# Float64 weights converted in pairs with ScalarE's help, and attention scores in four column-tiled strips

## The chip, the core and the metric

The kernel runs on one core of a Trainium2 chip. The metric is the device time of one execution in microseconds (us); the time of a kernel is the median of several executions. The engines are called as in the profile: PE (TensorE, matmuls), PEld (its weight loads), DVE (VectorE), ACT (ScalarE), POOL (GpSimd) and SP (SyncE, which here only issues DMAs). ACT and POOL have DMA queues too.

## What is computed

A linear recurrence over 768 steps (4 sequences, 8 heads, head size 48), a gated up/down layer with weights that come as float64, and a top-1 mixture of 8 experts. The reference, cut to what matters:

```python
# recurrence; complex decay a, only the real part of the state is read
for t in range(S):
    new_re = ar * S_re - ai * S_im
    new_im = ar * S_im + ai * S_re
    S_re, S_im = new_re + k[t] (x) v[t], new_im
    y[t] = q[t] @ S_re
x = (x @ w_a * (x @ w_b)) @ w_out          # 384 -> 1536 -> 384, float64 weights
e = argmax(x @ w_gate); p = softmax(x @ w_gate)[e]
out = p * (max(x @ w1[e], 0) @ w2[e])      # 8 experts, 384 -> 1024 -> 384
```

## The kernel before

**Stages.** The 3072 tokens go in 12 batches j of 256 tokens, three batches to a sequence, each batch in two chunks c of 128 tokens. A first phase takes each batch through the recurrence and the gated layer; a second one, from about 604 us on, runs the experts on tokens sorted by expert. The second phase is the same in both kernels but for the eviction of the very last tile.

**The recurrence of a chunk.** DVE, ACT and POOL make decayed keys and queries, which are written to DRAM and read back transposed as kT and qT by small DMAs (L1300; those of qT are issued by ACT, those of kT by SP). PE then makes, for each group hg of four heads, the scores `sc` (L1349: four matmuls 96x128 by 96x128 in fp32, which the trace shows as two records each); DVE multiplies them with a causal mask into `sm` (L1353); PE transposes the keys, `kn` (L1358, four heads a bank), which ACT copies to SBUF (L1363); PE makes `y` (L1388) from `sm` and v and from the state T and qT, in four column tiles of 32, and `kv` (L1408), the new addition to the state, also in column tiles of 32. ACT and DVE turn y into the high and low part of x (L1399, L1402), DVE updates the state from kv. Two small DVE copies (L1293, `column`) put the decay of a chunk beside q and A. The PSUM tiles of sc, kn, kv, of the folded gate weights (wt_p, wg_p) and of the expert counts (rk_p) share one ring of three banks, "sc".

**The gated layer.** Batch 0 runs in plain fp32 (`up32` L979, `down32` L985) since its weights are not yet split; later batches take f32r products in three terms, high x high, high x low and low x high (`up` L971 from xH, xL; `down` L1014 from gH, gL). Weights are cut into 12 slices f of 128 columns of w_a and w_b, and 128 rows of w_out. A float64 matrix slice of 128x384 is loaded by SP as pairs of 32-bit words (`raw`, L888, L890) and made into fp32 by three DVE operations: exponent and upper mantissa shifted (L897), low bits or-ed in (L900), sign or-ed in (L903). This is `conv`, 36 times. For w_out PE also transposes the slice and folds the gate weights into eight more columns (wt_p L916, wg_p L926, with ACT's copies L920 and L929). Later `parted` splits each slice into a high part (ACT, L953) and a low one: ACT writes -a into wL (L946) and a DMA of POOL's adds a rounded to it (L949).

**Order.** All of phase 1 is put in order by the class `Plan`. Each piece of work is added with an engine, a weight (its planned duration), a due time `at`, and what it reads and writes. `run` plays five queues forward with these weights and always emits the ready piece with the earliest due time. The table `TIMES` shifts due times by kind, with a pair (shift, stretch). Instructions then stand on each engine in the order emitted, and an engine works its own list strictly in that order. DMAs of SP and ACT carry one of eight semaphores in turn, so a DMA also waits for the one eight issues before it (DMAHW0 to 7 in the listings below).

Of the kernel before, what the change touches and what calls it, by code (L numbers as in the profile page):

```python
# [16 lines left out]
HP = 64  # L17
DM, DFF = 384, 1536
NF = DFF // 128
# [14 lines left out]
FH = 4  # L34
MH = (20.0, 3.0, 26.0, 3.0)
SPLIT = (70.0, 1.51, 6.0)
FIRST = (6, 3)
# [10 lines left out]
    ('pre', 0, 1, 0): (-32.6, 1),  # L48
    ('pre', 0, 1, 1): (18.2, 2.16),
    ('pre', 0, 0, 3): (6.7, 4),  # L50
    ('pre', 0, 0, 4): (12.1, 1),
    ('pre', 0, 1, 2): (-17.5, 1),
    ('pre', 0, 1, 3): (-26.8, 1),
    ('attn', 0, 'PE'): (-31.9, 1),
    'load': (-11.6, 1),
    'conv': (2, 1),
    'fold': (15.3, 0.43),
    ('pre', 1, 0, 0): (-21.7, 1),
    ('pre', 1, 0, 1): (-21.2, 1),
    ('turn', 1, 0): (-24.5, 1),  # L60
    ('pre', 1, 0, 3): (9, 1.54),
    ('attn', 1, 'PE'): (8, 1.03),
    ('gate', 0, (0,)): (-8.7, 1.46),
    ('down', 0, (0,)): (35, 1),
    ('up', 0, (0, 1)): (27, 1),
    ('down', 0, (0, 1)): (16.9, 0.28),
    'less': (-1.8, 0.8),
    'high': (-0, 0.89),
    ('pre', 2, 0, 0): (-70.8, 1),
    ('pre', 2, 0, 1): (-3.6, 0.35),  # L70
    ('pre', 2, 0, 2): (-32.9, 1),
    ('pre', 2, 0, 4): (-43.4, 1),
    ('up', 1): (35.8, 0.57),
    ('gate', 1): (-26.5, 0.3),
    ('attn', 2, 'PE'): (40.4, 0.51),
    ('v', 3): (-41, 1),
    ('down', 2): (15.5, 0.93),
    ('attn', 3, 'PE'): (33.2, 0.77),
    ('pre', 4, 0, 0): (39.6, 1),
    ('pre', 4, 0, 1): (-35.1, 1),  # L80
    ('pre', 4, 0, 3): (-31.5, 1),
    ('up', 3): (-5.1, 0.16),
    ('gate', 3): (93.4, 1),
    ('down', 3): (-11.7253, 1.2931),
    ('attn', 4, 'PE'): (4.8735, 1),
    ('attn', 4, 'DVE'): (-34.6, 1),
    ('attn', 4, 'ACT'): (-22.9, 1),
    ('up', 4): (-11.3, 1),
    ('gate', 4): (-41.3, 1),
    ('down', 4): (-9.1, 1),  # L90
# [5 lines left out]
F64_HI = float(np.uint32((1150 << 20) | 0xFF000).view(np.float32))  # L96

# [363 lines left out]
def fast(tc, q, k, v, a_re, a_im, w_a, w_b, w_out, w_gate, w1, w2, out, dram, x2d):  # L461
# [5 lines left out]
    with ExitStack() as mctx, ExitStack() as ctx:  # L467
# [9 lines left out]
        p_sc = sctx.enter_context(tc.tile_pool(name="p_sc", bufs=3, space=bass.MemoryType.PSUM))  # L477
# [376 lines left out]
        def pair(nm, f):  # L854
            return ("ab", f) if nm != "o" else ("o", f // 2)
# [4 lines left out]
        def width(nm):  # L860
            return 384 + (NE if nm == "o" else 0)
# [736 lines left out]
```

## Time and profile before

| | us |
|---|---|
| median of 3 runs | 896.99 (896.51 to 898.57) |
| the profiled execution | 897.96 |
| its span | 896.2 |
| PE busy in the span | 850.6 (95%) |
| DVE / ACT / POOL busy | 562.2 / 479.7 / 318.3 |

The profiled execution is 0.97 us above the median and 1.76 us longer than its span. PE's busy share counts overlapping records of a pipelined engine as one stretch, so 95% says that PE had work in flight for all but 45.6 us. In the profile's 40 slices PE stands at 0 and 3 in the first two and at 9 from then to the last but one; the granted clock is full in every slice. The chain of work that ended last is PE for 92% of the span.

### The profile page before, as it was taken

What the parts mean: (1) busy time and instruction counts of PE and PEld (TensorE: products, weight loads), DVE (VectorE), ACT (ScalarE), POOL (GpSimd) and SP (SyncE); (2) the same over time, 40 slices, a digit from 0 to 9 for tenths busy, and PEclk for the clock granted to TensorE, in tenths of its full rate; (3) what the DMA queues carried; (4) which work ended last, traced back from release to release, by engine and by line L of the source; (5) the groups of instructions that cost most, each with busy time, mean ns of one, the idle gap of its engine ahead of it and who ended that gap; (6) DMA issues with size and microseconds to landing.
All of it is one profiled execution on the core that took longest, in us unless ns stands there. A gap on an engine that the chain in (4) does not pass through costs nothing.

```text
span 896.2 us, 20677 instructions
## 1 busy us (share of the span) xinstructions
PE 850.6 (95%) x8186; PEld 815.9 (91%) x8186; DVE 562.2 (63%) x1285; ACT 479.7 (54%) x915; POOL 318.3 (36%) x309
## 2 busy tenths in 40 slices
PE   0399999999999999999999999999999999999997
PEld 0387899999999999999999999999999999999996
DVE  6999996775647567484939576345563655455541
ACT  6478787674746456564646473224452544444441
POOL 2341441323363636354353545221123223234111
PEclk9999999999999999999999999999999999999999
DMA  9999975242324272734354453403444454454510
GB/s 253 267 273 259 231 147 151 76 112 66 115 49 131 62 221 46 193 92 124 117 154 132 93 156 81 125 2 111 156 116 128 143 161 136 144 171 125 163 61 24
DMA packets 133017, 120.28 MB, mean 134 GB/s; under 512 B 35964, under 2 KB 127434, under 8 KB 132911
## 3 DMA queue, kind: packets, MB, share of 16 engines
q1 hardware_dynamic: 121519, 100.60, 39.7%
q0 software_dynamic: 9664, 17.47, 8.4%
q8 instruction: 66, 1.08, 0.5%
q10 hardware_dynamic: 1728, 0.79, 0.4%
q14 instruction: 40, 0.33, 0.1%
HBM read 82.48 MB, written 10.61 MB: 104 GB/s over the span
## 4 chain that ended last, share of the span: by engine, by line
PE 92%; DVE 3%; DMA 3%; SPq 1%; ACT 1%; issue 0%; POOL 0%; ACTq 0%; POOLq 0%
PE ab_p L971 31%; PE o L1014 16%; PE o L810 13%; PE h_p L778 12%; PE sc_p L1349 4%; PE y_p L1388 4%; PE ab_p L979 3%; PE o L985 2%; PE kv_p L1408 2%; PE kn_p L1358 1%; PE tn_p L755 1%; DMA q<-in_q_dram 1%; DMA qT<-A 1%; DMA raw<-in_moe_w_dram 1%; DMA raw<-in_moe_w_a_dram 1%; SPq L1138 0%
## 5 line engine op out<-in xcount | busy, mean ns | idle before, releaser
L971 PE MATMUL ab_p<-xH,wL 128*128 128x256 f32 x792 | 221.7, 280 | 0.0
L971 PEld LDWEIGHTS ab_p<-xH,wL 128*128 128x128 f32 x792 | 148.9, 188 | 0.0
L1005 POOL TENSOR_TENSOR gL<-g,gH 128x256 fp32r<-128x256 f32 x96 | 80.0, 835 | 172.3 <-ACT gH L1001 165.6
L994 ACT COPY g<-ab_p 128x256 f32<-128x256 f32 x132 | 48.9, 371 | 136.8 <-PE ab_p L971 124.0
L997 DVE TENSOR_TENSOR g<-g,ab_p 128x256 f32<-128x256 f32 (+1 forms) x148 | 60.5, 409 | 94.0 <-ACT g L994 92.0
L971 PE MATMUL ab_p<-xH,waH 128*128 128x256 f32 x396 | 114.0, 288 | 0.0
L971 PE MATMUL ab_p<-xL,waH 128*128 128x256 f32 x396 | 111.4, 281 | 0.0
L971 PE MATMUL ab_p<-xL,wbH 128*128 128x256 f32 x396 | 110.9, 280 | 0.0
L971 PE MATMUL ab_p<-xH,wbH 128*128 128x256 f32 x396 | 110.8, 280 | 0.0
L1014 PE MATMUL o<-woH,gH 128*128 128x392 f32 x264 | 96.5, 365 | 0.0
L1014 PE MATMUL o<-wL,gH 128*128 128x392 f32 x264 | 90.0, 341 | 0.0
L1014 PE MATMUL o<-woH,gL 128*128 128x392 f32 x264 | 89.9, 341 | 0.0
L810 PE MATMUL o<-w2H,h 128*128 128x384 f32 (+3 forms) x312 | 86.4, 340 | 0.0
L778 PE MATMUL h_p<-sH,w1H 128*128 128x256 f32 (+6 forms) x240 | 77.4, 322 | 0.2 <-DVE hL L789 0.2
L778 PE MATMUL h_p<-sH,w1L 128*128 128x256 f32 (+6 forms) x240 | 76.9, 321 | 0.0
L778 PE MATMUL h_p<-sL,w1H 128*128 128x256 f32 (+6 forms) x240 | 76.8, 320 | 0.0
L971 PEld LDWEIGHTS ab_p<-xH,waH 128*128 128x128 f32 x396 | 74.8, 189 | 0.9 <-issue 0.2
L1001 ACT ACTIVATE gH<-g 128x256 fp32r<-128x256 f32 x132 | 54.5, 413 | 38.5 <-DVE g L997 35.3
L971 PEld LDWEIGHTS ab_p<-xL,waH 128*128 128x128 f32 x396 | 74.7, 189 | 0.4
L971 PEld LDWEIGHTS ab_p<-xH,wbH 128*128 128x128 f32 x396 | 75.0, 189 | 0.0
L971 PEld LDWEIGHTS ab_p<-xL,wbH 128*128 128x128 f32 x396 | 74.8, 189 | 0.0
L824 POOL DMA_INDIRECT out_dram<-ye,ids x29 | 29.9, 1032 | 112.1 <-ACT ye L823 99.9
(211 smaller groups left out, 2135.8 us busy)
## 6 DMA issues: line engine op xcount, KB each, us to landing
raw<-in_moe_w_dram SPq DMA_DIRECT2D x64, 384.0 KB, 3.4
x2d<-x SPq DMA_DIRECT2D x24, 196.0 KB, 3.3
q<-in_q_dram SPq DMA_DIRECT2D x24, 192.0 KB, 4.5
v<-in_v_dram SPq DMA_DIRECT2D x24, 192.0 KB, 4.1
raw<-in_moe_w_a_dram SPq DMA_DIRECT2D x12, 384.0 KB, 6.8
raw<-in_moe_w_b_dram SPq DMA_DIRECT2D x12, 384.0 KB, 5.4
raw<-in_moe_w_out_dram SPq DMA_DIRECT2D x12, 384.0 KB, 7.4
wL<-a POOLq DMA_DIRECT2D x24, 192.0 KB, 6.8
```

What stands on the lines that cost most here:

```text
L778: nc.tensor.matmul(out=t, lhsT=lh[:, o:o + 128], rhs=rh[:, kk], start=n == 0, stop=n == 8)
L810: nc.tensor.matmul(out=G["o", c], lhsT=lh, rhs=rh, start=f == 0 and n == 0, stop=f == NH - 1 and n == len(ops) - 1)
L824: d = nc.gpsimd.indirect_dma_start(out, bass.IndirectOffsetOnAxis(ap=ids[0:r, c:c + 1], axis=0), y[0:r], None, bounds_check=NT - 1, oob_is ...
L971: nc.tensor.matmul(out=t[:, i], lhsT=lh[:, kk * 128:(kk + 1) * 128], rhs=rh[:, kk], start=n == 0, stop=n == 8)
L979: nc.tensor.matmul(out=t[:, i], lhsT=A32[nm, f][:, kk * 128:(kk + 1) * 128], rhs=xT["F", 0][:, kk, cs[0]:cs[0] + len(cs)].rearrange("p c t ...
L994: nc.scalar.copy(out=G["g", j, f], in_=G["ab", j, f][:, 0])
L997: nc.vector.tensor_tensor(out=G["g", j, f], in0=G["g", j, f], in1=G["ab", j, f][:, 1], op=ALU.mult)
L1001: nc.scalar.activation(out=G["H", j, f], in_=G["g", j, f], func=ACTF.Copy)
L1005: eng.tensor_tensor(out=G["L", j, f], in0=G["g", j, f], in1=G["H", j, f].bitcast(F32), op=ALU.subtract)
L1014: nc.tensor.matmul(out=G["o", j, c], lhsT=lh[:, c * C:(c + 1) * C], rhs=rh, start=f == first and n == 0, stop=f == last and n == 2)
L1349: nc.tensor.matmul(out=S["p", hg][:, h], lhsT=pq["k", j][:, hg * 4 + h, c, :], rhs=pq["q", j][:, hg * 4 + h, c, 0:C], start=True, stop=True)
L1388: nc.tensor.matmul(out=t[q4 * 32:q4 * 32 + 32, kk], lhsT=a, rhs=b, start=f0, stop=f1)
```

## The change

1. **Conversion in pairs** (`conv`). The slices of w_a and w_b of one f lie side by side in a tile "ab" of 768 columns; w_out keeps its own. The three DVE operations become one ACT operation and two of DVE: ACT scales the low word into a float whose low mantissa bits carry it (`tail`, L934), DVE shifts the high word and xors (`body_`, L937), then or-s it with a constant and xors (`head`, L940). 24 units (12 of 768, 12 of 384 columns) instead of 36.
2. **Splitting** (`parted`). For f below 9 ACT makes the high part in one operation and DVE subtracts (`taken`, L1008); no ACT negation and no POOL DMA. For f from 9 on the old way stays, with 768 columns for ab.
3. **Scores in strips**, for batches j from 3 on (`sc`, L1454). The keys of a head are taken in four strips of 32, and a strip's matmul covers only the queries from its own first one on: 128, 96, 64 and 32 columns. The strips of the four heads of a group go to four different column tiles. Scores lie in two banks kept for them, zeroed once (`emptied`); since a head's strips are rotated by r, v has three rotated copies `vrot`, loaded by six small DMAs of SP a chunk, and the mask is a rotated 128x4x128 tile in bf16, built on POOL at the start.
4. **Banks.** From j=3 on kn, kv and rk share the single bank that is left (ring "s1").
5. **Sessions**, from j=3 on. Column-tiled work stands together on PE: the scores of chunk 0; y and kv of chunk 0 with the scores of chunk 1; y and kv of chunk 1.
6. **Smaller things.** The `column` copies go from DVE to ACT; the last tile's eviction is one ACT operation instead of a half on ACT and a half on DVE; the PSUM pool of phase 2 is opened anew; a new `TIMES` table (43 entries became 61), so that the order of phase 1 changes throughout.

```diff
-    for hg in range(2):
-        add("PE", 0.9, at_(sc, hg), qk + [("kT", c), ("qT", c)], [("sc_p", j, c, hg)], take="sc")
...
+    for b in range(0, C, STRIP):
+        for r in range(4):
+            a = (b + r * STRIP) % C
+            nc.tensor.matmul(out=t[a:a + STRIP, r, b:C], lhsT=pq["k", j][:, hg * 4 + r, c, b:b + STRIP], rhs=pq["q", j][:, hg * 4 + r, c, b:C], start=True, stop=True)
...
+    if c == 0:
+        add("PE", 1.54, both, qk + [("kT", 0), ("qT", 0)], P_)
+    else:
+        rest, after, r_, w_ = pending.pop()
...
+        add("PE", 4.05 - (0.9 if first_b else 0), joined, r_ + qk + [("kT", 1), ("qT", 1)], w_ + P_, take=ring(j))
...
+        add("PE", 2.7 if not last else 1.95, lambda rest=rest: [f() for f in rest], r_, w_, **({} if last else dict(take=ring(j))))
...
-        P = Plan({"sc": 3})
+        P = Plan({"sc": 3, "s1": 3 - KEPT})
...
+            def tail():
+                held()
+                nc.scalar.activation(out=K["a"].bitcast(F32), in_=K["lo"], func=ACTF.Copy, scale=TAIL[0], bias=TAIL[1])
+            def body_():
+                nc.vector.scalar_tensor_tensor(out=K["a"], in0=K["hi"], scalar=3, in1=K["a"], op0=ALU.logical_shift_left, op1=ALU.bitwise_xor)
+            def head():
+                nc.vector.scalar_tensor_tensor(out=K["a"], in0=K["hi"], scalar=0x7FFFFFFF, in1=K["a"], op0=ALU.bitwise_or, op1=ALU.bitwise_xor)
...
+            def taken():
+                nc.vector.tensor_tensor(out=W["L", nm, f], in0=A32[nm, f], in1=W[nm, f][0], op=ALU.subtract)
...
-                        nc.vector.tensor_copy(out=(ld[x, j] if x == "q" else PT[x, j])[:, :, lo:hi, C:C + 1], in_=T("A")[:, :, :, C - 1:C])
+                        nc.scalar.copy(out=(ld[x, j] if x == "q" else PT[x, j])[:, :, lo:hi, C:C + 1], in_=T("A")[:, :, :, C - 1:C])
...
-                            elif e == NE - 1 and c == nt - 1:
-                                nc.scalar.activation(out=y[0:r, 0:DM // 2], in_=G["o", c][:, 0:DM // 2], func=ACTF.Copy, scale=gt[0:r, c])
-                                nc.vector.tensor_scalar(out=y[0:r, DM // 2:DM], in0=G["o", c][:, DM // 2:DM], scalar1=gt[0:r, c], scalar2=None, op0=ALU.mult)
...
     'load': (-11.6, 1),
-    'conv': (2, 1),
+    'load': (3.846, 0.5624),
+    'conv': (119.1, 0.419),
```

How instructions stand now at three places. (waits DMAHW3) names the semaphore of the DMA that a DMA waits for.

SP's queue in the first 40 us, before: the transposed keys of chunk 0, then the next weight loads (raw).

```order
L1300 DMA kT<-Bt 16x8x128 [waits DMAHW0_49]
L1300 DMA kT<-k 16x8x128 [waits DMAHW1_49,DVE_49]
L1300 DMA kT<-k 16x8x128 [waits DMAHW3_49]
L1300 DMA kT<-k 16x8x128 [waits DMAHW4_49]
L890 DMA raw<-in_moe_w_a_dram 128x3x256 [waits DMAHW6_49]
```

And after:

```order
L1390 DMA kT<-Bt 16x8x128 [waits DMAHW2_49]
L915 DMA raw<-in_moe_w_a_dram 128x3x256 [waits DMAHW3_49]
L1390 DMA kT<-k 16x8x128 [waits DMAHW5_49,DVE_49]
L1390 DMA kT<-k 16x8x128 [waits DMAHW7_49]
L1390 DMA kT<-k 16x8x128 [waits DMAHW0_49]
```

A weight load now stands between the two groups of transposed keys, and it takes the semaphore DMAHW3.

ACT's queue at the same place, before: the last three transposed queries of chunk 0 (qT<-q) between small activations.

```order
L1300 DMA qT<-q 16x8x129 [waits DMAHW2_49,DVE_49]
L1275 ACTIVATE X<-X 128x3x128 [waits DVE_49]
L1300 DMA qT<-q 16x8x129 [waits DMAHW5_49]
L1187 ACTIVATE X<-X,biases 128x3x128 [waits Activation_49]
L1187 ACTIVATE X<-X 128x3x128 [waits DVE_49]
L1300 DMA qT<-q 16x8x129 [waits DMAHW7_49]
```

And after:

```order
L975 COPY a_294<-wg_p 128x8 [waits PE_49]
L1390 DMA qT<-A 16x8x129 [waits DMAHW4_49]
L1390 DMA qT<-q 16x8x129 [waits DMAHW6_49]
L1286 ACT_TABLE_LOAD
L1390 DMA qT<-q 16x8x129 [waits DMAHW1_49]
L1390 DMA qT<-q 16x8x129 [waits DMAHW3_49]
```

The last of the three now waits for DMAHW3, which the weight load above holds.

PE in the steady part, batch 3, before: y and kv of a chunk, with nothing of the next chunk beside them (o is the down projection, ab_p the up projection).

```order
L1388 MATMUL y_p<-sm,v_182 32x128 x16
L1408 MATMUL kv_p<-v_182,kn 32x48 x24
L1014 MATMUL o_2413<-woH_1554,gH 128x392
L1014 MATMUL o_2413<-wL,gH 128x392
```

And after, where the scores of the next chunk follow as strips, 16 matmuls for each group of four heads:

```order
L1498 MATMUL y_p<-sm,vr_169 32x128 x8
L1518 MATMUL kv_p<-v_164,kn 32x48 x24
L1454 MATMUL scores<-qT,kT 32x128 x4
L1454 MATMUL scores<-qT,kT 32x96 x4
L1454 MATMUL scores<-qT,kT 32x64 x4
L1454 MATMUL scores<-qT,kT 32x32 x4
L1454 MATMUL scores<-qT,kT 32x128 x4
L1454 MATMUL scores<-qT,kT 32x96 x4
L1454 MATMUL scores<-qT,kT 32x64 x4
L1454 MATMUL scores<-qT,kT 32x32 x4
L1076 MATMUL o_2322<-woH_1620,gH 128x392
```

Counted over the whole of PE's list, the column-tiled places of batches 3 to 11 (a run of y, kv or strips with no other matmul inside) are 32 before and 27 after; the 36 groups of old scores stand apart from them.

## Rows read from the trace of the kernel before

**Rows 1.** Windows of the span: stretch, length, busy us by engine (instructions)

```profile
39.36:118.47 79.11, 77.44 (x1018) 64.26 (x1019) 75.38 (x160) 61.92 (x130) 29.22 (x31) 1.00 1.05 252
186.00:604.20 418.20, 418.20 (x4615) 407.38 (x4617) 259.31 (x582) 224.37 (x408) 184.00 (x168) 1.00 0.40 109
```

**Rows 2.** Timeline of the start: start, length, engine, line, operation, tiles, count

```profile
33.02 0.58 ACTq L1300 DMA_DIRECT2D qT<-q  x1
33.42 0.59 SPq L890 DMA_DIRECT2D raw<-in_moe_w_a_dram  x1
39.41 0.56 ACTq L1300 DMA_DIRECT2D qT<-A  x1
39.36 3.76 PE L1349 MATMUL sc_p<-qT,kT 96*128 96x128 f32 x16
```

**Rows 3.** DMA issues, 30 to 46 us: tiles, queue, count, KB, us to landing

```profile
qT<-q ACTq DMA_DIRECT2D x6, 64.5 KB, 4.3
```

**Rows 4.** Timeline of PE, one group of old scores among down-projection matmuls

```profile
146.66 1.05 PE L1349 MATMUL sc_p<-qT,kT 96*128 96x128 f32 x8
147.47 0.42 PE L1014 MATMUL o<-woH,gH 128*128 128x392 f32 x1
147.73 0.34 PE L1014 MATMUL o<-wL,gH 128*128 128x392 f32 x1
```

**Rows 5.** Timeline of PE, the end of a y and the matmul behind it

```profile
389.69 0.40 PE L1388 MATMUL y_p<-sm,v 128*32 128x128 f32 x8
389.91 0.40 PE L1388 MATMUL y_p<-qT,T 96*32 96x128 f32 x8
390.24 0.44 PE L1014 MATMUL o<-woH,gH 128*128 128x392 f32 x1
```

**Rows 6.** Timeline of PE, a kv between up and down projections

```profile
393.26 0.28 PE L971 MATMUL ab_p<-xL,wbH 128*128 128x256 f32 x1
393.38 0.28 PE L971 MATMUL ab_p<-xH,wL 128*128 128x256 f32 x1
393.58 0.88 PE L1408 MATMUL kv_p<-v,kn 128*32 128x48 f32 x48
394.39 0.45 PE L1014 MATMUL o<-woH,gH 128*128 128x392 f32 x1
394.69 0.34 PE L1014 MATMUL o<-wL,gH 128*128 128x392 f32 x1
394.87 0.34 PE L1014 MATMUL o<-woH,gL 128*128 128x392 f32 x1
```

**Rows 7.** Timeline of PE, the folded gate weights: 24 records of 8 columns

```profile
67.70 0.38 PE L926 MATMUL wg_p<-wg,wt 128*32 128x8 f32 x24
68.00 0.60 PE L985 MATMUL o<-a,g 128*128 128x392 f32 x1
```

**Rows 8.** Groups, DVE to 118 us, ACT to 140: busy us, mean ns

```profile
L903 DVE SCALAR_TENSOR_TENSOR a<-raw,a 128x384 uint32<-128x384 uint32 x36 | 19.4, 549 | 0.0
L897 DVE TENSOR_SCALAR a<-raw 128x384 uint32<-128x384 uint32 x36 | 13.7, 401 | 1.0 <-DMA raw<-in_moe_w_a_dram 1.0
L1221 DVE SCALAR_TENSOR_TENSOR X<-X,re 128x768 f32<-128x768 f32 x2 | 1.9, 946 | 0.0
L1187 ACT ACTIVATE X<-X 128x768 f32<-128x768 f32 x6 | 5.1, 844 | 0.0
```

**Rows 9.** Timeline of the last eviction, and of a whole one

```profile
881.25 0.58 ACT L823 ACTIVATE ye<-o,gt 128x384 f32<-128x384 f32 x1 [1.12 <-PE o L810]
889.62 0.42 ACT L818 ACTIVATE ye<-o,gt 120x192 f32<-120x192 f32 x1 [7.79 <-PE o L810]
890.08 0.42 DVE L819 TENSOR_SCALAR ye<-o,gt 120x192 f32<-120x192 f32 x1 [4.01 <-ACT ye L818]
```

**Rows 10.** Timeline of PE and ACT, a transposed key group and its copy

```profile
257.69 0.49 PE L1358 MATMUL kn_p<-ident,kT 96*128 96x96 f32 x4
258.23 0.48 ACT L1363 COPY kn<-kn_p 128x384 f32<-128x384 f32 x1 [0.32 <-PE kn_p L1358]
```

More of the change, by code (lines that the diff above doesn't have):

```diff
@@ L79 @@
[L79 to L90, printed above, removed]
+    ('pre', 0, 1, 0): (70.2, 1),
+    ('pre', 0, 0, 2): (-165.1, 1),
+    ('turn', 0, 0): (-39.1, 1),
@@ new lines @@
+    ('up', 0, (0, 1)): (-121.9, 1),
+    'less': (259.2, 0.1),
+    'taken': (227.4, 4.8374),
+    ('pre', 2, 0, 3): (-399.9, 1),
+    ('up', 1): (-107.7, 4),
+    ('gate', 1): (-311, 1),
+    ('down', 1): (-48, 4),
+    ('attn', 2, 'PE'): (-179.2, 3.45),
+    ('pre', 3, 0, 0): (301.3, 1),
+    ('up', 2): (232.2, 1.84),
+    ('gate', 2): (-209.7, 1),
+    ('down', 2): (80.1, 0.0409),
+    ('attn', 3, 'PE'): (-61.8, 3.4866),
+    ('pre', 4, 0, 1): (214, 1),
+    ('pre', 4, 0, 2): (58.1, 1),
+    ('pre', 4, 0, 3): (55.9, 1),
@@ new lines @@
+    ('pre', 4, 0, 4): (220.3, 1),
+    ('down', 3): (-113.2, 1),
+    ('attn', 4, 'PE'): (40.3, 1),
+    ('attn', 4, 'DVE'): (185.4, 1),
+    ('up', 4): (38.3, 1),
+    ('gate', 4): (-289.3, 1),
+    ('down', 4): (41.4, 1),
+    ('attn', 1, 'DVE'): (-92.4, 1),
+    ('attn', 1, 'ACT'): (96.3, 1),
+    ('down', 0, (0, 1)): (82.3, 1),
+    ('pre', 2, 0, 0): (60.8, 1),
+    ('pre', 2, 0, 1): (-215, 1),
+    ('attn', 3, 'DVE'): (47.3, 1),
+    ('pre', 4, 0, 0): (430.6, 1),
+    ('up', 3): (15.7, 3.97),
@@ L632, in count @@
                     base = eoff
-                t = p_sc.tile([128, 2, NE], F32, tag="sc", name="rk_p")
+                t = bank([128, 2, NE], "rk_p")
                 for c in range(2):
@@ L1304, in mul @@
                     for x in "Aq":
-                        add("DVE", column(x), ks("A", x), [("column", x, lo)], weight=0.16)
+                        add("ACT", column(x), ks("A", x), [("column", x, lo)], weight=0.2)
                 add(e, times, ks(src, "Cc" if c2 == 0 else "F"), ks(t))
@@ L1425, in at_ @@
                     return lambda: f(*a)
-                for hg in range(2):
-                    add("PE", 0.9, at_(sc, hg), qk + [("kT", c), ("qT", c)], [("sc_p", j, c, hg)], take="sc")
-                    add("DVE", on("DVE", 512), at_(mask, hg), [("sc_p", j, c, hg)], [("sm", hg)], give=True, alone=False)
-                if not last:
-                    for hg in range(2):
-                        add("PE", 0.33, at_(kn, hg), qk + [("kT", c)], [("kn_p", j, c, hg)], take="sc")
-                        add("ACT", on("ACT", 384, True), at_(kept, hg), [("kn_p", j, c, hg)], [("kn", 0), ("kn", 1)] if hg == 0 else [("kn", 1)], give=True)
```

355 lines of the change are left out of this document (234 added, 121 removed).

## The prediction, made before the changed kernel ran

> **What bounds the kernel now.** I read the windows by stage first, since the 95% of PE is a mean over stages with different limits. From 39.36 us on PE is the wall: in the stretch to 118.47 it is busy for 77.44 of 79.11 us, and from 186.00 to 604.20 for all of 418.20 [rows 1]. The list of PE's waits says the same: its long entries all end before 39.4 us, and the chain of waits is PE for nearly all of the rest. In the steady stretch DVE has 259.31 and ACT 224.37 of 418.20 us, so work moved between these two is worth nothing there. Between 39.36 and 118.47, however, DVE is busy 75.38 of 79.11: there it is as full as PE, and a queue in the wrong order could become the wall. So three things can move the end: PE work taken out after 39 us, the moment at which PE starts its stream, and new gaps in it. For PE I read the timeline as distances from start to start, because records overlap and their own lengths say little.
>
> **Scores in strips.** An old group of four heads is eight records; from its start to the next matmul 0.81 us pass, and the down-projection matmul behind it needs 0.26 until the next one starts [rows 4], where an undisturbed one takes 0.18 [rows 6]. Batches 3 to 11 have 9 x 2 x 2 = 36 such groups, of which the order shows 34 followed by such a matmul: 36 x 0.81 + 34 x 0.08 = 31.9 us.
>
> A new group is four sets of eight records (four column tiles, two records to each matmul as in fp32 now), with 128, 96, 64 and 32 columns. No strip is in the trace. Its nearest rows are y, kv and the folded gate weights, all in column tiles of 32: eight records of 128 columns take 0.22 [rows 5]; 48 records of 48 columns 0.81, so eight 0.135 [rows 6]; 24 records of 8 columns 0.30, so eight 0.10 [rows 7]; the latter two include leaving the mode. The set of 96 columns is then 0.165 by proportion, that of 64 columns 0.11 to 0.135, that of 32 columns 0.10 to 0.135, in all 0.595 to 0.655. I take 0.605, near the lower end since kv's and the gate weights' prices hold an exit. 36 x 0.605 = 21.8 (at most 23.6; if cost were columns alone, 0.55 and 19.8). The strips save **10.1 us** (8.3 to 12.1).
>
> **Sessions.** Entering column tiles costs 0.20 instead of 0.12 before kv, leaving them 0.30 instead of 0.18 behind it [rows 6], and y's last set holds 0.33 instead of 0.22 [rows 5]: 0.08 + 0.12 + 0.11 = 0.31 for one visit. 32 visits become 27: 5 x 0.31 = 1.6 saved. Inside a session strips follow kv or one another with new operands; between nothing and an entry's 0.08 for each of the 36 groups I take half, 1.4 lost. Net 0.2 saved (1.6 saved to 1.3 lost).
>
> **The single bank.** From batch 3 on, 30 kn groups, 15 kv and 9 rk share one bank, 54 users. A group's copy on ACT ends 258.23 + 0.48 - 257.69 = 1.02 us after the group began [rows 10]. In the new order six down-projection matmuls (6 x 0.18 = 1.1 us) or a whole up projection stand between two users, so the bank is free just in time when ACT is prompt; when ACT has a longer operation in hand, PE waits for the rest of it. That wait is behind PE's next kn, so everything on PE is queued behind it. Bound: zero to 0.5 us (about one ACT operation) each; I take 0.03 on average, 1.5 us in all, for this and every other small new stall.
>
> **The start.** SP's new order puts a weight load between the two groups of chunk 0's transposed keys, and ACT's last qT<-q of the chunk now carries the semaphore which that load holds. Before, the load issued at 33.42 let the qT<-A eight issues later go only at 39.41, 6.0 us on [rows 2]. The load moves ahead of three issues of some 0.59, to 31.7, or 32.3 with POOL's longer preamble in front of the keys; the last query is then issued at 32.3 + 6.0 = 38.3, not at 33.02, and lands 4.3 us later [rows 3], at 42.6. The first scores began at 39.36 [rows 2]: 3.2 us late. Of that some comes back: of PE's 79.11 - 77.44 = 1.67 us idle behind it [rows 1] most, since the weights are then ready, and one more pair of transposes and gate weights (about 0.6) is done before instead of behind. Net **+1.0** (-1 to +4).
>
> **Conversion and splitting.** Before, 36 x (2 x 0.549 + 0.401) = 54.0 us of DVE (L900 runs like L903); after, 24 wide operations of 0.946 and 24 narrow ones of 0.549, 35.9 us [rows 8]. `taken` gives 9 x (0.946 + 0.549) = 13.5 back. So DVE has about 4.6 us less of these, all hidden as long as PE is the wall; in the start, where DVE is as full as PE, this is its margin. ACT takes 12 x (0.844 + 0.48) = 15.9 for `tail` and drops 72 operations of some 0.48 for 9 x 1.32 + 3 x 2 x 1.32 = 19.8: 34.6 against 35.7, even [rows 8, 10]. Priced at nothing; without PE's cover they would cost the lateness of the first up projection, which is rival B. The POOL DMAs that go (27 slices) and the 108 small v loads lie beside PE in a stage with free queues; priced at nothing too. What stands behind those loads on SP is later loads only, planned tens of us ahead.
>
> **The last eviction.** The two halves run one after the other, 889.62 to 890.08 + 0.42 = 890.50; a whole one takes 0.58, to 890.20 [rows 9]. 0.3 saved, on the path.
>
> **Sum.** 897.96 - 10.1 - 0.2 - 0.3 + 1.0 + 1.5 = 889.9 for an execution like the profiled one, which is 0.97 above the median: **889.0**.
>
> **Rivals.**
> A. Short matmuls have a floor. If no set of strips were cheaper than the widest, 0.22, a group would cost 0.88 and 36 of them 31.7: the gain of strips is gone, 889.0 + 36 x (0.88 - 0.605) = 898.9. Against it: eight records cost 0.135 at 48 columns and 0.10 at 8 [rows 6, 7]. The Trainium skill (TensorEngine Tiling (Array Packing), Performance Considerations, Instruction Overhead) says that each matmul has about 60 cycles of overhead on TRN2, so that one column lasts as long as 60. Read as 25 ns of issue for each record that would be an estimate of 0.2 a set, 0.82 a group and 896.7 us; the trace disagrees, with 13 ns a record for 24 in 0.30 us [rows 7]. 5%.
> B. The start slips further. If queries come later still, or DVE (75.38 of 79.11 busy) has the wrong conversion at its head when PE asks for it, the whole stream moves; at 4.5 more than taken, 893.5. For it: DVE now waits in line for kv of chunk 0 before the next conversions, and by my count the last up weights are ready only some 1.5 us ahead of PE. 12%.
> C. The single bank stalls PE, the slower side. With a mean wait of 0.25 us, half an ACT operation of 0.48, 54 users cost 13.5, of which 1.0 is in the sum: 901.5. It cancels the gain from 0.03 + 8.0 / 54 = 0.18 us on. For it: 1.02 us against 1.1 leaves no slack. Against it: ACT is busy for only 224.37 of 418.20 [rows 1], and its copy here waited 0.32 for PE, not PE for it [rows 10]. 9%.
> D. The change doesn't do what it says to the time: new order and waits give back what PE saves, place by place, with no single cause, 897. 4%.
>
> **How the numbers follow.** My forecast has 70%. Its own bounds: with 19.8 for strips, no loss inside sessions, a start 1 us early and no stalls, 889.0 - 2.0 - 1.4 - 2.0 - 1.5 = 882.1; with 23.6, 1.4 more inside sessions, a start 4 us late and 2 us more of stalls, 889.0 + 1.8 + 1.4 + 3.0 + 2.0 = 897.2. All at once is unlikely, so the low end is 883; the upper end, 897, also takes in B and most of D. Left out are C, A and the edges. A measurement of this kernel can tell about 0.2% from no change, so faster is below 895.2 and slower above 898.8: faster 0.70 + 0.12 = 0.82; same, D and half of A, 0.07; slower, C and the rest, 0.11.
>
> **What the profile of the changed kernel would show.** Strips: from the first to the next matmul behind a pair of groups about 1.2 us, sets getting shorter from 0.22 to about 0.1; at 0.8 a group, A. Sessions: 27 visits. Bank: PE's waits with kn_p, kv_p or rk_p behind ACT's copies summing to about a microsecond; over 8 us, C. Start: first scores near 42.6 and the load ahead of the last query; batch 0's up projections without waits for the conversion, or else B. PE's windows from there on without idle time; the last eviction one ACT operation of 0.6. The forecast is wrong if PE is idle by several us in the steady part, or if a strip's set costs the same whatever its columns.

## The result, and the profile after

The changed kernel takes 881.96 us (median of 5, 880.94 to 882.99) against 896.99 for the kernel before in the same session (median of 5, 896.51 to 898.75): ratio 0.9823, 95% interval 0.9808 to 0.9838. That is 15.0 us faster. I had forecast 889.0, 8 us faster, with a range of 883 to 897. The sign was right; the gain was nearly double, and the time fell out of the range at its low end.

The head of the page of the changed kernel: span and PE's busy time.

```profile
span 880.0 us, 22475 instructions
...
PE 833.7 (95%) x9050; PEld 803.0 (91%) x9050; DVE 565.0 (64%) x1218; ACT 486.6 (55%) x923; POOL 291.6 (33%) x295
```

The span is 16.2 us shorter than in the profiled execution before, 1.2 more than the medians are apart. PE's share is the same 95%: what went is PE's work, not its idle time. The windows of the changed kernel (stretch, length, busy time of PE, PEld, DVE, ACT and POOL, granted clock, DMA share, GB/s), to be held against [rows 1]; the second ends 16.2 us earlier than the one there, the third is the expert phase:

```profile
40.66:118.47 77.81, 76.63 (x993) 63.49 (x994) 69.98 (x121) 63.22 (x117) 8.33 (x8) 1.00 0.70 196
...
186.00:588.00 402.00, 400.55 (x5509) 392.68 (x5509) 265.40 (x565) 229.77 (x424) 181.56 (x168) 1.00 0.47 122
630.67:873.48 242.81, 242.81 (x1481) 236.07 (x1480) 125.25 (x299) 102.03 (x210) 65.68 (x61) 1.00 0.41 128
```

PE is the wall from its first scores on, as before: 76.63 of 77.81 us in the first stretch, where it had 77.44 of 79.11; and 400.55 of 402.00 in the steady stretch. DVE still stands at 69.98 of 77.81 in the first. PE's waits in the changed kernel (what waited, for whom, us in total, times, longest):

```profile
PE wt_p L962 <- DVE a L940: 35.0, 4, 27.1
PE wg_p L972 <- ACT wt L966: 2.6, 4, 0.9
PE rk_p L670 <- DVE oh L647: 0.8, 1, 0.8
PE sc_p L1449 <- PE o L1076: 0.6, 1, 0.6
PE ab_p L1030 <- issue: 0.5, 1, 0.5
PE scores L1454 <- DMA q<-in_q_dram: 0.2, 1, 0.2
```

Only the last four lie behind 118.47 us, 2.1 us in all, and three of them (1.45 us) make up the idle time of the steady stretch. The kernel before had four short waits too (1.1, 0.5, 0.5 and 0.2), but two of them lie in the start, one at 144.62 and one in the expert phase; in its steady stretch PE had none [rows 1]. So small new stalls did come. None is a wait for the single bank's copies, the mechanism of my slower rival C: not one kn, kv or rk waits for ACT.

Where the 16.2 us come from, by summing PE's distances from start to start over each kind of matmul in both traces (good to a tenth or two, since some records are missing or counted twice where the trace is cut; differences are taken before rounding):

| | before | after | difference | forecast |
|---|---|---|---|---|
| first instruction of PE | 26.27 | 27.07 | +0.8 | |
| scores, kn, y, kv of batches 0 to 2 | 32.4 | 30.1 | -2.3 | |
| transposes, gate weights, fp32 projections | 70.5 | 69.8 | -0.7 | |
| **start, sum** | | | **-2.2** | **+1.0** |
| scores of batches 3 to 11 | 28.9 | 23.1 | -5.8 | |
| y, kv, kn of batches 3 to 11 | 52.4 | 50.1 | -2.3 | |
| projections beside other work, over their usual pace | 13.0 | 10.3 | -2.8 | |
| **strips, sessions, bank, sum** | | | **-10.9** | **-8.8** |
| usual pace of up and down projections | 420.2 | 417.6 | **-2.5** | **0** |
| expert phase and end | | | **-0.8** | **-0.3** |

The first experts' matmul stands at 646.14 before and 630.67 after, so on PE the first phase lasts longer than to the 604 us at which the stages were divided above. In what follows I use the start of that matmul beside the medians: in four of the sixteen traces, one of the kernel before among them, the expert phase has a wait of 1 to 2 us of its own (last section), which can blur a median by as much. In five traces with the changed kernel's order on all engines (the changed kernel, e7, e11, e12, e13) that start lies between 629.21 and 631.78, so a difference of a microsecond or two says nothing.

### The profile page after: what moved, and what is told of

It is laid out like the page before. It is cut to its first block, busy times and chain, and to the rows that moved or that the text cites. A ratio compares the mean times of both kernels' runs of the same rounds, so it can differ in the third digit from the quotient of the medians.

```text
span 880.0 us, 22475 instructions
## 1 busy us (share of the span) xinstructions
PE 833.7 (95%) x9050; PEld 803.0 (91%) x9050; DVE 565.0 (64%) x1218; ACT 486.6 (55%) x923; POOL 291.6 (33%) x295
## 4 chain that ended last, share of the span: by engine, by line
PE 82%; issue 8%; DVE 3%; DMA 3%; POOL 2%; ACT 1%; SPq 0%; POOLq 0%; ACTq 0%
PE ab_p L1030 31%; PE o L1076 16%; PE o L843 9%; PE h_p L811 9%; PE y_p L1498 5%; PE scores L1454 2%; PE kn_p L1463 2%; PE sc_p L1449 2%; PE ab_p L1038 2%; PE kv_p L1518 2%; PE o L1044 1%; PE tn_p L788 1%; POOL out_dram L854 1%; DVE a L937 1%; DMA raw<-in_moe_w_b_dram 1%
## 5 line engine op out<-in xcount | busy, mean ns | idle before, releaser
L1030 PE MATMUL ab_p<-xH,wabH 128*128 128x256 f32 x792 | 223.4, 282 | 0.5 <-issue 0.5
L1030 PE MATMUL ab_p<-xL,wabH 128*128 128x256 f32 x792 | 221.2, 279 | 0.0
L1030 PEld LDWEIGHTS ab_p<-xH,wabH 128*128 128x128 f32 x792 | 149.9, 189 | 0.4
L1030 PEld LDWEIGHTS ab_p<-xL,wabH 128*128 128x128 f32 x792 | 148.8, 188 | 0.5 <-issue 0.4
L1059 DVE TENSOR_TENSOR g<-g,ab_p 128x256 f32<-128x256 f32 x132 | 55.1, 417 | 116.3 <-ACT g L1056 116.1
L1076 PE MATMUL o<-woH,gH 128*128 128x392 f32 x264 | 93.8, 355 | 0.0
L822 DVE SCALAR_TENSOR_TENSOR h<-h_p,h 128x384 fp32r<-128x384 f32 (+1 forms) x48 | 26.7, 556 | 62.4 <-ACT h L820 62.2
L820 ACT ACTIVATE h<-h_p 128x384 fp32r<-128x384 f32 (+4 forms) x48 | 24.5, 511 | 76.4 <-PE h_p L811 76.4
L843 PE MATMUL o<-w2L,h 128*128 128x384 f32 (+3 forms) x168 | 56.7, 338 | 0.0
L843 PEld LDWEIGHTS o<-w2H,h 128*128 128x128 f32 (+3 forms) x312 | 56.3, 185 | 0.5
```

The source lines that it names most:

```text
L820: nc.scalar.activation(out=hH, in_=t, func=ACTF.Relu)
L822: nc.vector.scalar_tensor_tensor(out=hL, in0=t[:, 0:main], scalar=0.0, in1=hH[:, 0:main].bitcast(F32), op0=ALU.max, op1=ALU.subtract)
L843: nc.tensor.matmul(out=G["o", c], lhsT=lh, rhs=rh, start=f == 0 and n == 0, stop=f == NH - 1 and n == len(ops) - 1)
L1030: nc.tensor.matmul(out=t[:, i], lhsT=lh[:, kk * 128:(kk + 1) * 128], rhs=rh[:, kk], start=n == 0, stop=n == 8)
L1059: nc.vector.tensor_tensor(out=G["g", j, f], in0=G["g", j, f], in1=G["ab", j, f][:, 1], op=ALU.mult)
L1076: nc.tensor.matmul(out=G["o", j, c], lhsT=lh[:, c * C:(c + 1) * C], rhs=rh, start=f == first and n == 0, stop=f == last and n == 2)
```

## The experiments

### e0: is the difference one of the execution that was profiled?

The kernel before, traced a second time.

> The kernel before, unchanged, for a second trace of it. In its first trace an undisturbed up projection started every 0.1175 us, in the changed kernel's every 0.1164, evenly over the whole stream; over 2376 of them that is 2.6 us, and 0.6 us more in the unchanged expert phase. Theory P (that difference is only the execution that happened to be profiled): this trace shows 0.1165 to 0.117 and an expert phase as long as the changed kernel's. Rival (something that runs beside PE in the kernel before slows every matmul): 0.1175 again.

It has its first expert matmul at 645.84 (646.14 in the first trace) and the same pace of undisturbed up projections, 0.1171 us in both, against 0.1162 in the changed kernel. So the pace belongs to the kernel, and theory P is out. Its span, 899.0, is longer than the first one's by 2.8 us for a wait in the expert phase and the lower clock behind it (last section).

### e1: strips alone undone

```diff
-                    if j < SWAP:
+                    if True:
                         for h in range(4):
...
-                    nc.vector.tensor_tensor(out=S["s", hg], in0=S["p", hg], in1=masks if j >= SWAP else causal.unsqueeze(1).to_broadcast([128, 4, C]), op=ALU.mult)
+                    nc.vector.tensor_tensor(out=S["s", hg], in0=S["p", hg], in1=causal.unsqueeze(1).to_broadcast([128, 4, C]), op=ALU.mult)
...
-                                if h % 4 and j >= SWAP:
+                                if False:
```

> The changed kernel with the four strips undone alone: scores of batches 3 to 11 as four full matmuls again, mask and v unrotated, but sessions, banks, conversion and planned times as in the changed kernel. Theory: strips are worth 36 x (0.81 - 0.625) = 6.7 us on PE, where a group of strips measured 0.625; 888.7. Rival 1 (strips are nearly the whole gain of 15): 894 or more. Rival 2 (sessions and order are the gain, strips little): below 885.

893.59 us (ratio to before 0.9939, interval 0.9917 to 0.9962); first expert matmul at 640.12, 9.5 later than in the changed kernel. PE's order is the changed kernel's here. The strips are worth more than I expected in this run, and about the 10.1 of the prediction; the timeline says why. A pair of head groups as strips, in the changed kernel (start, length, instruction):

```profile
233.87 1.32 PE L1454 MATMUL scores<-qT,kT 96*32 96x128 f32 x64
235.12 0.45 PE L1076 MATMUL o<-woH,gH 128*128 128x392 f32 x1
```

1.25 us from its start to the next projection, 0.625 a group, where I had forecast 0.605. The same work as full matmuls behind a kv, in the experiment:

```profile
241.84 0.86 PE L1518 MATMUL kv_p<-v,kn 128*32 128x48 f32 x48
242.63 2.05 PE L1449 MATMUL scores<-qT,kT 96*128 96x128 f32 x16
244.44 0.36 PE L1030 MATMUL ab_p<-xH,wabH 128*128 128x256 f32 x1
```

1.81 us a pair, 0.56 more; for 18 pairs that is 10.1. It is not the session that makes full scores dear. A pair with no kv ahead of it, between a small rank matmul and a down projection of the same run:

```profile
419.02 2.03 PE L1449 MATMUL scores<-qT,kT 96*128 96x128 f32 x16
420.81 0.42 PE L1076 MATMUL o<-woH,gH 128*128 128x392 f32 x1
```

That is 1.79. In the kernel before a lone group takes 0.81, but the projection behind it holds 0.08 more [rows 4], so two of them come to 1.78. My 6.7 had left out those 0.08, which the prediction's 31.9 holds: 36 x (0.89 - 0.625) is 9.5.

### e2: sessions alone undone

```diff
-                if j >= SWAP:
+                if False:
                     P_ = [("scores", i) for i in range(KEPT)]
...
-                if c == 0 and j < SWAP and j + 1 < NB:
+                if c == 0 and j + 1 < NB:
```

> The changed kernel with the sessions undone alone: strips for each group of four heads, y and kv planned singly again, by the planner's older rule with 0.64 for a strip group. In the order the column-tiled visits of the whole kernel become 67 instead of 45. Theory: a visit costs 0.31, so 22 x 0.31 = 6.8 us more, 888.8. Rival 1 (a visit costs far less where the planner puts it well, sessions are worth nothing): 882 to 884. Rival 2 (visits cost more than the rows show, 0.5 or more): 893 or more.

888.23 us (0.9876, 0.9832 to 0.9920); first expert matmul at 637.69, 7.0 later than in the changed kernel. PE's waits are the same as there to half a microsecond, and what grew are the steps of y, kv and kn and of the projections next to them. So I put the 7.0 us down to visits: 0.32 for each of the 22, near the 0.31 that I had read from [rows 5, 6]. Both rivals miss the time. The planner dealt the order anew in this run, so the price of a visit is not shown apart from that; no wait of PE speaks for another cause.

### e3: strips, sessions and banks undone together

```diff
-SWAP, KEPT = 3, 2
+SWAP, KEPT = 12, 2
```

> The changed kernel with parts 3 to 5 undone together: full scores, three shared banks, no sessions; conversion, splitting and planned times as in the changed kernel. Theory: strips 6.7, five visits more at 0.31 and fifteen fp32 visits more at 0.083 give 9.5 us, 891.5; the other 5.5 us of the gain then lie in the start, the conversion and the order. Rival (all the gain is in parts 3 to 5, the rest is neutral): 897.

897.40 us (0.9981, 0.9961 to 1.0002); first expert matmul at 643.88, 13.2 later than in the changed kernel and only 2.0 to 2.3 ahead of the kernel before. The rival was nearer than my expectation. But the order was dealt anew here too, under due times made for other work, so that nearly all of the gain hangs on parts 3 to 5 is not shown by this run alone. What it does show: up projections keep the quick pace of the changed kernel, 0.1161 us, without strips, sessions and banks, and over 2376 of them that is 2.4 us, as much as this run is ahead of the kernel before.

### e4 and e8: conversion undone, first with a new order, then with the order kept

```diff
-BY_TAIL = {"ab": 0, "o": 0}
+BY_TAIL = {}
```

> The changed kernel with the conversion undone alone: three DVE operations again (shift, low bits, sign) on the same 768- and 384-wide tiles, no ACT operation; the planner puts the order anew around them. DVE gets 12 x 0.55 + 12 x 0.40 = 11.4 us more before about 100 us, where it is as full as PE. Theory S (the start lost nothing because DVE got room): the conversion falls behind, PE waits for the weights of batch 0, 4 to 8 us more in the first stage, 886 to 890. Rival (DVE's share there is slack, the start is set by the transposed queries alone): within 1 us of the changed kernel. Pace of plain up projections if the layout of the weights decides it: unchanged, 0.116.

908.89 us (1.0115, 1.0089 to 1.0140): 27 us slower than the changed kernel, far more than either theory said. Two windows of its first stage (columns as above):

```profile
105.00:120.00 15.00, 8.19 (x57) 6.09 (x52) 13.54 (x30) 12.56 (x19) 2.25 (x2) 0.71 0.76 191
120.00:135.00 15.00, 12.44 (x245) 11.48 (x246) 13.56 (x22) 10.94 (x20) 4.49 (x3) 0.73 0.37 89
```

PE is idle for 6.8 of the 15 us from 105 on, and the granted clock of that window and the next is 0.71 and 0.73 of full speed. But the planner had dealt the whole order anew, for due times that were made for other work, so this could not be laid at the conversion's door. The second try emits the changed kernel's own order, with the three DVE operations put where the two stood:

```diff
 def tail():
     held()
-    nc.scalar.activation(out=K["a"].bitcast(F32), in_=K["lo"], func=ACTF.Copy, scale=TAIL[0], bias=TAIL[1])
 def body_():
-    nc.vector.scalar_tensor_tensor(out=K["a"], in0=K["hi"], scalar=3, in1=K["a"], op0=ALU.logical_shift_left, op1=ALU.bitwise_xor)
+    nc.vector.tensor_scalar(out=K["a"], in0=K["hi"], scalar1=0x07FFFFFF, scalar2=3, op0=ALU.bitwise_and, op1=ALU.logical_shift_left)
+    low()
 def head():
-    nc.vector.scalar_tensor_tensor(out=K["a"], in0=K["hi"], scalar=0x7FFFFFFF, in1=K["a"], op0=ALU.bitwise_or, op1=ALU.bitwise_xor)
+    sign()
```

> The changed kernel with the conversion undone as in e4, but in the changed kernel's own order: where ACT had its operation stands none, where DVE had the first of two stand shift and low bits, where the second, the sign. PE's list is that of the changed kernel to the letter. DVE is busy 70.1 of the 75 us from 45 to 120 in the changed kernel and gets some 11 more. Theory S (DVE sets the start too): slack of 4.9 is used up, PE waits, 3 to 8 us slower, part of it at half clock. Rival (e4's 27 us were all DVE, not order): 15 us or more. Rival 2 (DVE is slack): below 1 us.

891.72 us (0.9932, 0.9909 to 0.9955); first expert matmul at 640.66, 10.0 later. PE's list is word for word the changed kernel's, so this is the price of DVE's extra passes in that order. Some of PE's waits (idle time before, for whom, in brackets):

```profile
41.11 0.88 PE L962 MATMUL wt_p<-ident,a 128*128 128x128 f32 x3 [7.94 <-DVE a L930]
...
69.14 0.52 PE L962 MATMUL wt_p<-ident,a 128*128 128x128 f32 x3 [1.16 <-DVE a L930]
...
96.70 5.45 PE L1038 MATMUL ab_p<-x,a 128*128 128x256 f32 x24 [2.25 <-DVE g L1052]
```

PE's waits for DVE's `a` in wt_p grow by 4.8 us (1.4 of it ahead of PE's first instruction), those for DVE's gates by 3.6, one for a DMA by 1.1, and ACT's copies hold it 0.9 less: 8.6 of the 10.0. Theory S holds, with a larger size: in the start PE stands behind DVE's conversions and gates, and the part that I had priced at nothing is worth 10 us in this order. The other 17 of e4's 27 us were the order.

### e5 and e9: splitting undone, likewise twice

```diff
-DIRECT = 9
+DIRECT = 0
```

> The changed kernel with the splitting undone alone: for every slice ACT negates, a DMA of POOL's adds, ACT makes the high part. ACT gets 18 operations more, DVE loses 13.5 us. Theory: hidden behind PE, within 1.5 us of the changed kernel; the pace of plain up projections after 140 us stays at 0.116, since nothing differs there but who wrote the weights. Rival: the direct subtraction is what lets the first f32r batches start on time, 3 us or more slower.

944.27 us (1.0520, 1.0475 to 1.0565), 62 us slower. With the order kept:

```diff
 def high():
+    if f < DIRECT:
+        less()
     w = wts.tile([128, n], F32R, tag=f"h{nm}{f}", name=f"w{nm}H{f}")
     nc.scalar.activation(out=w, in_=A32[nm, f], func=ACTF.Copy)
-    if f < DIRECT:
-        place()
...
 def taken():
-    nc.vector.tensor_tensor(out=W["L", nm, f], in0=A32[nm, f], in1=W[nm, f][0], op=ALU.subtract)
+    rest()
```

> The changed kernel with the splitting undone as in e5, in the changed kernel's own order: ACT negates and rounds back to back, a DMA of POOL's adds where DVE subtracted. ACT gets 18 operations, some 12 us, before 140 us; DVE loses 13.5. Theory: e5's 62 us were the planner's new order, not the splitting; here within 2 us of the changed kernel. Rival: ACT's 12 us delay gates and copies that PE waits for, 5 us or more.

904.58 us (1.0065, 1.0042 to 1.0088), 23 slower; first expert matmul at 650.97, 20.3 later. My theory was right that e5's 62 us were mostly the order (some 40 of them), and wrong on the rest. PE's longest waits behind the first scores:

```profile
PE kn_p L1463 <- ACT a L975: 6.0, 1, 6.0
PE ab_p L1030 <- DMA wL<-a: 3.3, 2, 2.8
```

6.0 us of kn behind ACT's copy beside the weights and 3.3 for the DMA that adds into wL; 2.2 of kv behind ACT's copy of kn follow two lines further on. ACT's extra operations, and the DMA, stand in PE's way. The clock pays too: 0.77 granted from 105 to 120 us, where PE was idle for 6.0 us, and 0.95 as a mean from 45 to 120.

### e6 and e10: the weight load among the transposed keys, likewise twice

```diff
-                t = loaded(i + x)
+                t = loaded(i + x) + (8 if (i, x) == (15, 0) else 0)
```

> The changed kernel with the one weight load that stood between the two groups of chunk 0's transposed keys put behind chunk 1's keys. In the changed kernel that load was issued at 32.88, the last transposed query that shares its semaphore went at 37.7 and the first scores began at 40.66. Theory: without it the query goes 3 to 4 us earlier and the first scores begin at 38 to 39, bound by the third pair of weight transposes at 38.3; the whole gets 0 to 1.5 us faster. Rival (scores are bound by DVE and the weights, not by the query): first scores at 40.5 again.

892.41 us (0.9944, 0.9926 to 0.9961), 10 slower, with the order dealt anew and new waits for qT (5.2 us in three lines of PE's list). First scores at 40.57. With the order kept, and the load moved in SP's list alone:

```diff
         for x, n, _ in out:
+            if n == late:
+                held = 1
+                continue
             ops[n]["f"]()
+            if held and ops[n]["e"] == "SP":
+                held += 1
+                if held == 4:
+                    ops[late]["f"]()
+                    held = 0
```

> The changed kernel with only that one weight load issued behind chunk 0's transposed keys; all four other engines keep their lists. e6 did it by due times, and the planner re-dealt the whole order (10 us slower). Theory: the last transposed query goes 3 us earlier, first scores at 38.8 to 39.5 instead of 40.66, the whole 0 to 1.5 us faster. Rival (the query is bound by ACT's list ahead of it, a table load and the weights' copies): first scores at 40.5, no difference.

882.00 us (0.9816, 0.9794 to 0.9839): no difference. First scores at 41.12, not at 39. The chain of waits at the start of the changed kernel (start, us, what):

```profile
32.88 4.80 DMA raw<-in_moe_w_a_dram
...
37.69 1.92 DMA qT<-q
39.61 0.47 ACT wt L966
...
40.13 0.51 PE wg_p L972 x24
...
40.66 3.75 PE sc_p L1449 x16
```

The hold that I had forecast is there: the load from 32.88 keeps the last transposed query of chunk 0 back until 37.69, and the weights' copy and fold stand behind it in ACT's list. In the experiment (its line numbers are ten higher) that query goes right behind the moved load, 2.0 us earlier; start, length and instruction of both issues, the time from the query's issue to its landing, and what stands ahead of the scores:

```profile
35.37 0.60 SPq L925 DMA_DIRECT2D raw<-in_moe_w_a_dram  x1
35.65 0.62 ACTq L1400 DMA_DIRECT2D qT<-q  x1
...
qT<-q ACTq DMA_DIRECT2D x1, 64.5 KB, 5.1
...
38.30 0.88 PE L972 MATMUL wt_p<-ident,a 128*128 128x128 f32 x3 [6.98 <-DVE a L950]
39.21 0.48 ACT L976 COPY wt<-wt_p 128x384 f32<-128x384 f32 x1 [3.19 <-PE wt_p L972]
39.74 0.51 PE L982 MATMUL wg_p<-wg,wt 128*32 128x8 f32 x24 [0.57 <-ACT wt L976]
41.12 1.19 PE L1459 MATMUL sc_p<-qT,kT 96*128 96x128 f32 x4 [0.87 <-DMA qT<-A]
```

The query now takes 5.1 us to land where it took 2.0, with the load in flight beside it, and lands at 40.71. That the load's bytes delay it is likely and not shown. The issue was freed and the data came no sooner, so ACT's list (the rival) did not bind either. And an earlier query could have won little: PE's fold, directly ahead of the scores, ends at 40.25 even here, because its transposes waited for DVE's conversion until 38.30. My 38.8 to 39.5 was out of reach. The trace puts PE's last wait, from 40.25 to 41.12, down to a query of chunk 1, which the code does not name as an input of these scores; the last 0.4 us of it stay open.

### e7, e11, e12, e13: what decides the pace of up projections

In each trace, 132 runs of 18 up projections go at one of two paces, near 0.114 or near 0.118 us a matmul. Before, 33 runs are of the fast sort, after 53. The slow ones average 0.1177 in both, the fast ones 0.1144 before and 0.1135 after: 33 x 18 x 0.0033 is 2.0 us, 53 x 18 x 0.0042 is 4.0, and the 2.0 between them are nearly all of the 2.1 us that up projections gained. Two kernels (e7, e11) shift SBUF addresses by an unused tile of 32 or 1056 bytes a partition (8 columns in the diff, 264 in the other); e12 is the changed kernel once more; e13 makes a transpose on PE twice at the very start.

```diff
+        const.tile([128, 8], F32, name="gap")
         zeros = const.tile([128, BT], F32, name="zeros")
```

> The changed kernel with an unused tile of 8 columns ahead of the zeros, so that SBUF addresses behind it move and nothing else does. Runs of 18 up projections go at one of two paces, 0.114 or 0.118, the same ones in every trace of a kernel. Theory A (addresses decide): other runs are fast in this trace. Theory B (the place in PE's list decides): the same runs are fast, mean 0.1162 again.

> As e7, with a gap of 1056 bytes a partition in place of 32. In e7 four fifths of the 18-matmul runs kept their pace. Theory A (addresses decide which runs take 0.114 and which 0.118, on a scale above 32 bytes): another pattern over slices. Theory B: the same slices are fast.

> The changed kernel unchanged, for a second trace. In its first trace 53 of 132 runs of 18 up projections went at 0.114 a matmul, the others at 0.118; in two traces of the kernel before the same runs were fast but for one or two. If the pattern belongs to the program, at least 120 of 132 runs keep their pace here; if a fifth of them change, as with the shifted tiles of e7 and e11, those told nothing of addresses.

```diff
-                for kk in range(3):
+                for kk in ([0] * (f == 0) + [0, 1, 2]):
                     nc.tensor.transpose(K["t"][:, kk], A32[nm, f][:, kk * C:(kk + 1) * C], ident)
```

> The changed kernel with one transpose of the first weights made twice, ahead of everything else on PE; all later instructions stand one place further on. Theory C (the place of an instruction in PE's list, counted from its start, decides the pace): other runs are fast than in the changed kernel's two traces, half of them changed. Theory D (what stands around the run decides): the pattern stays.

Two traces of the kernel before agree on the sort of 131 of the 132 runs; two of the changed kernel on 127. One matmul more at the start leaves 130 as they were: it is not the count from the list's start (theory C falls, D stands). Shifted addresses leave 108 and 111, so addresses move up to a sixth of the runs (e10, at unchanged addresses, leaves 123), while the mean stays at 0.1161 to 0.1164 and the single times, 880.72 and 883.20, are the changed kernel's. Between the kernel before and the changed one only 68 agree. In both traces an up run that stands directly behind another one with a down run ahead of that is seldom fast (1 of 8 after, 2 of 14 before), but a run behind six down projections, an up run and six more is fast 24 times in 60 after and twice in 28 before, and the busy time of DVE, ACT and POOL beside a run goes with its pace only weakly (no line of theirs is correlated above 0.4). Parts 1 to 5 of the change, undone, leave most of the gain: 55 runs are fast in e3, 48 in e8, 46 in e9. So the pace goes with the program, and the new order is what is left of the change to account for most of it; that is argued, and what in an order decides the pace stays open.

## Why the prediction was off, step by step

The rows of the table miss the forecast by 3.2 us in the start, 2.1 in strips, sessions and bank, 2.5 in the pace and 0.5 in the expert phase and the end, all the same way.

**Right: the wall.** PE from its first scores on, before and after; steady waits small; ACT and DVE of no weight behind 186 us.

**Right: strips and the price of a visit.** A strip group measured 0.625 for my 0.605 (bounds 0.595 to 0.655), 0.64 as the mean of all 36. From start to start the sets of 128, 96, 64 and 32 columns take 0.24, 0.17, 0.11 and 0.06 us (first group of a pair, median of nine pairs without a kv ahead), so a set's cost falls with its columns, and rival A is out. One visit measured 0.32 for 0.31. The Trainium skill (TensorEngine Tiling (Array Packing), Key Properties) says that a change of the tiling mode drains the engine; these runs agree, and put the price at about 0.32 us for going in and out. The floor in my rival A (the same page of the Trainium skill, Performance Considerations, Instruction Overhead: about 60 cycles a matmul, by my estimate 25 ns) is one of a matmul, and I had read it as one of a record. The trace shows two records for each matmul here, so my 13 ns a record did not answer it: the 12 matmuls of [rows 7] come to 25 ns each. The four matmuls of a 32-column set do, with 15 ns each.

**Wrong in size: the inside of a session.** I had charged half an entry for each of 36 groups, 1.4 us. The end of a y, its kv and the strips behind it in a joined session:

```profile
240.61 0.40 PE L1498 MATMUL y_p<-sm,vr 128*32 128x128 f32 x8
240.84 0.40 PE L1498 MATMUL y_p<-qT,T 96*32 96x128 f32 x8
241.06 0.82 PE L1518 MATMUL kv_p<-v,kn 128*32 128x48 f32 x45
241.68 0.30 PE L1454 MATMUL scores<-qT,kT 96*32 96x128 f32 x1
```

The last set of y now takes 0.22 to the kv, where it held 0.33 ahead of a projection [rows 5]; kv, all but its last three records, takes 0.62 to the first strip, where it took 0.81 to a projection [rows 6]. A change of operands inside column tiles costs nothing here, and each joint saves a whole exit: the 1.4 did not come. **The single bank** and every other new stall were charged with 1.5 us. None of the bank's kind came, but other new waits of 1.45 us did, in the steady stretch, so that term was right in size by luck. Together strips, sessions and bank gave 10.9 us for 8.8 forecast.

**Wrong in mechanism and in sign: the start.** I had let the last transposed query set the first scores. In both kernels PE's own chain did: the transposes of a w_out slice, which wait for DVE's conversion, ACT's copy, the fold, and the scores directly behind it. Before, it is the second slice:

```profile
37.35 0.90 PE L916 MATMUL wt_p<-ident,a 128*128 128x128 f32 x3 [7.65 <-DVE a L903]
38.29 0.48 ACT L920 COPY wt<-wt_p 128x384 f32<-128x384 f32 x1 [0.90 <-PE wt_p L916]
38.82 0.51 PE L926 MATMUL wg_p<-wg,wt 128*32 128x8 f32 x24 [0.57 <-ACT wt L920]
39.40 0.17 ACT L929 COPY a<-wg_p 128x8 f32<-128x8 f32 x1 [0.63 <-PE wg_p L926]
...
raw<-in_moe_w_a_dram SPq DMA_DIRECT2D x1, 384.0 KB, 3.9
```

After, the third one:

```profile
38.33 0.87 PE L962 MATMUL wt_p<-ident,a 128*128 128x128 f32 x3 [6.98 <-DVE a L940]
39.60 0.48 ACT L966 COPY wt<-wt_p 128x384 f32<-128x384 f32 x1 [3.55 <-DMA qT<-q]
```

Scores began at 40.66, 1.3 later than before, for a forecast 3.2. Of that 0.9 is the conversion, which DVE ended later, one slice further on, and 0.4 is the hold, which let ACT's copy start only at 39.60; in e10 it followed the transposes directly, at 39.21. In e7 and e13, with the changed kernel's order, the held query went at 37.22 and 37.09 instead of 37.69, the copy followed the transposes directly, and scores began at 40.33 and 40.41. So nearly all of the hold lies behind DVE's conversion, and it moves the scores by 0 to 0.4 us. Its terms were too large as well, 4.80 us measured for 6.0, and 1.92 for a landing of 4.3. The 6.0 was a misreading: the load issued at 33.42 (last line of the first listing) had landed after 3.9 us, at 37.29, and the qT<-A at 39.41 stood in ACT's list behind the copy at 39.40, which waits for PE's fold. The 4.3 came from the kernel before, whose DMA share from 30 to 45 us was 0.94, where the changed kernel's was 0.72. The part that comes back was 3.5 us for 2.2: first y and kn run at full pace sooner (y of chunk 0 in 0.90 us instead of 1.56), and the wait for x is gone. In all 3.2 us off, the largest single miss.

**Unproven: conversion and splitting at nothing.** I had compared busy times and found a small surplus. With the order kept, undoing them costs 10 and 20 us of the first phase: the new order rests on them, and I had noted myself that DVE was as full as PE there and then gave that no price. But this is what they are worth inside the new order, not a term that the sum lacks. Against the kernel before, e3, which has them without parts 3 to 5, is ahead by no more than the pace of its up projections is worth. With its order dealt anew that doesn't settle it, and what the two are worth as a term of the sum stays open. Their own durations were near: DVE's passes over the changed kernel's slices,

```profile
L937 DVE SCALAR_TENSOR_TENSOR a<-raw,a 128x768 uint32<-128x768 uint32 x12 | 12.9, 1077 | 0.0
L940 DVE SCALAR_TENSOR_TENSOR a<-raw,a 128x768 uint32<-128x768 uint32 x12 | 11.4, 947 | 0.0
```

with the narrow ones (7.4 and 6.6 us) 38.3 us against 35.9 forecast, since the pass that follows ACT's took 1.08 where I had 0.946; and ACT's, which took 0.93 for 0.844:

```profile
L934 ACT ACTIVATE a<-raw 128x768 f32<-128x768 uint32 x12 | 11.1, 927 | 3.1 <-DMA raw<-in_moe_w_b_dram 3.1
```

**Not foreseen: the pace** of plain projections, 2.5 us. The trace of the kernel before has both sorts of runs, but not how many would be fast in another order; the cause is open.

**The last eviction** is whole and 0.58 us long:

```profile
873.52 0.58 ACT L853 ACTIVATE ye<-o,gt 120x384 f32<-120x384 f32 x1 [7.79 <-PE o L843]
874.41 1.05 POOL L854 DMA_INDIRECT out_dram<-ye,ids  x1 [3.19 <-ACT ye L853]
```

The scatter behind it starts 1.27 us after the start of PE's last matmul, where it was 1.56: the 0.3 that I had forecast. From there to the span's end it is 5.55 us for 5.44, so 0.2 remains.

**The range.** My own bounds came to 882.1, just above what was measured; I cut them to 883 as unlikely "all at once". They needed not all be at once, because the start, which I had let come 1 us early at most, came 2.2 early, and the pace was in no bound.

## What to carry to other kernels

Price work in another tiling mode by the visit, not only by the matmul: here 0.31 to 0.32 us for going in and out, nothing for changing operands inside, so pieces that share a mode are worth joining. Before a DMA is made the cause of a start, look at what stands directly ahead of it on the waiting engine: here that was PE's own fold, and the held query moved it by 0.4 us at most. A stage in which a second engine is as full as the bounding one has no free edits: what is taken from that engine is worth what the order can make of it, and in these runs that showed only with the order held still. Where a table of planned times sets the order, undo a part with the order kept as well as by its switch; the same three edits cost 27, 62 and 10 us when the order was dealt anew and 10, 23 and 0 when it was not.

## What the runs showed of the chip

Up projections of one shape go at two paces, 0.114 and 0.118 us, constant over a run of 18 and the same from execution to execution of one kernel.

A query that went 0.28 us behind a 384 KB load took 5.1 us to land (e10); issued after the load had landed, it took 2.0.

A short wait of PE can cost twice its length. In the second trace of the kernel before, PE waited 1.76 us near the start of the experts, behind ACT, whose conversion of an expert's weights stood waiting for its load. The matmuls that follow it (start, length, instruction):

```profile
670.37 0.39 PE L778 MATMUL h_p<-sH,w1H 128*128 128x256 f32 x1 [1.76 <-DVE hL L789]
...
673.70 0.41 PE L778 MATMUL h_p<-sH,w1H 128*128 128x256 f32 x1
673.91 0.41 PE L778 MATMUL h_p<-sL,w1H 128*128 128x256 f32 x1
...
674.82 0.28 PE L778 MATMUL h_p<-sH,w1H 128*128 128x256 f32 x1
674.94 0.28 PE L778 MATMUL h_p<-sL,w1H 128*128 128x256 f32 x1
```

0.21 us apart at 673.70 and 0.12 from 674.82 on, for the same shape: half speed for some 3.5 us, from about 671 on. The granted clock of the 20 us window from 665.84 on is 0.91, in its neighbours 1.00; by the same measure e4's window at 0.71 holds 6.8 us of idle time of PE, and the one at 0.73 follows it. The same wait was 1.99 us long in e1, with a granted clock of 0.91 behind it, and 1.25 in e3, 1.32 in e6 and 0.18 in the first trace of the kernel before, where the clock stayed at 1.00.
